# Last pooled queries as quarter products, diagonals by one GpSimd multiplication, and a new written-out order

## The chip, the cores and the metric

The kernel runs on one NeuronCore of a Trainium2 chip. The metric is the device time of one execution in microseconds; lower is better. The time of a kernel is the median of several executions. The engines are named as in the profile: PE is TensorE (PEld its loading of weights), DVE is VectorE, ACT is ScalarE, POOL is GpSimd, SP is SyncE, which here issues all DMAs.

## What is computed

Eight batches of eight heads, 576 positions, 64 elements per head. Each head goes through two attentions, whose sum is the input of a mixing layer:

```python
q_d = q.reshape(B, H, S // 4, 4, D).mean(axis=3)      # k_d, v_d likewise
out_up = np.repeat(sm_attn(q_d, k_d, v_d), 4, axis=2)  # attention among 144 pooled positions
mask = np.abs(pos[:, None] - pos[None, :]) < 4         # local attention, 7 keys per query
out_local = softmax(where(mask, q @ k.T / 8, -1e9)) @ v
x = (out_up + out_local) as (B, S, 512)
xk = mu_k * x + (1 - mu_k) * x_prev                    # xr likewise with mu_r
out = sigmoid(xr @ w_r) * (relu(xk @ w_k) ** 2 @ w_v)
```

All arrays are float32. The weights are 512x512 (`w_r`), 512x1024 (`w_k`) and 1024x512 (`w_v`).

## The kernel before, in words

Two heads make a pair; there are 32 pairs (n = 0 to 31), four to a batch. Positions of all batches are 4608 rows, cut into ten chunks of 512 or 256 rows (c = 0 to 9). A chunk needs the attention output of its rows, so pairs run ahead of chunks and both are interleaved on TensorE.

**A pair.** q and k are loaded (`load_raw`, L489) and turned; for pairs 0 to 4 TensorE turns them (`flip`, L537), later VectorE. GpSimd pools four neighbours of q into `qd` (`pool_q`, L589), of k into `kd` (`pool_k`, L604), and of v into `vd` (`pool_v`, L614). `score_pe` (L636) makes the local scores in many small matmuls: 96 passes for a pair below 8, 48 from pair 8 on. The pooled scores are 144 queries by 144 keys for each head e. Queries 0 to 127 come from `down_part_pe` (L711), four 64x64 products for the four quarters of the array (e is the quarter's rows, h its columns; "D" in the lists below). The last 16 queries come in one of two ways: for pairs 0 to 8 `last_q` (L597, ScalarE, two copies) puts them beside zeros in columns 144 to 271 of `qd`, and `down_last` (L706) makes one product with all 128 rows, two passes (line 709); for later pairs `down_part_pe` with h = 2 takes queries 80 to 143 of each head as two more quarter products ("L").

**Quarters.** `quarters(n, m, last)` (L822) makes four lists, one for each quarter of the array, with the value products of pair n (W: 48 columns, U and T: 144 columns) and the pooled scores of pair m (D, L). It issues them interleaved by planned time, so that the four quarters work side by side. With `last` true the L entries are left out. Softmax then goes over VectorE, ScalarE and GpSimd (`down_top`, `down_exp`, `down_sum`, `down_norm`, `score_top` to `spread`); `down_turn` (L754) turns the result back for pairs below 8. `av_out` (L887) writes the pair's part of x.

**Who calls them.** `score_both` (L852) for pairs 0 to 4 makes `down_last`, scores, four quarters; `down_alone` (L858) does so without scores for pair 8; `run_pe` (L863) makes a run of scores of pair n with values of pair n-1: for n = 5 to 7 in the order `down_last`, quarters, scores; from 8 on scores, quarters with L.

**A chunk.** `mix_prev` and `mix_part` form xk and xr, `mix_high` and `mix_low` split them into two parts for full accuracy; `k_pe` (L951), `v_pe` (L997) and `r_pe` (L983) are 12, 6 and 12 matmuls of up to 512 columns. The first chunk's xk is made on TensorE by `mix_pe` (L931) from eight diagonal matrices 128x128 that `diagonals` (L405) makes on ScalarE from the identity and `mus`; `mus` come from `load_mus`, `turn_mus` (TensorE) and `copy_mus` (ScalarE). The 20 weight parts (`fetch_weight`, 512 KB each) are split by `weight_scale` to `weight_low` (L447 to L481).

**Order.** Every step is added to a plan (`Plan.add`, L142) with its engine, an estimated time and a due time. `ORDER` (L47) is a written-out order of all 1995 steps: two characters for one step, its number in order of adding. `arrange` (L273) takes it, assigns PSUM banks, and computes planned times; each engine then issues its own steps in that order, five queues in all. `fill` (L333) puts throw-away matmuls (`keep_warm`, L471, line 475) where the plan has TensorE wait in the first 100 us. A queue never overtakes: a step that waits holds all behind it on its engine.

Of the kernel before, what the change touches and what calls it, by code (L numbers as in the profile page):

```python
# [17 lines left out]
P = 128  # L18
# [65 lines left out]
OtOuOvOwO)O*O-O4O3OxOyO,O+O/O.
# [9 lines left out]
class Plan:  # L94
# [18 lines left out]
    GROW = dict(DVE=1.03, ACT=1.02, POOL=1.05, SP=1.1)  # L113
# [244 lines left out]
def attention_moe(ctx: ExitStack, tc, q, k, v, mu_k, mu_r, w_k, w_v, w_r, band, ident, out):  # L358
# [14 lines left out]
    qds = [cp.tile([P, 272], F32, name=f"qd{i}") for i in range(2)]  # L373
# [332 lines left out]
    def down_last(n):  # L706

        d = st[n]
        nc.tensor.matmul(down_boards[n][:, D0 + DP:D0 + DP + 144], d["qd"][:, 144:272], d["kd"], start=True, stop=True)

# [7 lines left out]

    def down_pe(n):
        for e in range(2):  # L720
            for h in range(2):
                down_part_pe(n, e, h)
# [637 lines left out]
```

## Time and profile before

| | us |
|---|---|
| median of 3 runs | 652.75 |
| lowest and highest | 652.3, 652.94 |
| the profiled execution | 653.26 |
| its span, first to last instruction | 651.1 |

| engine | busy us of the span | share |
|---|---|---|
| PE | 631.3 | 97% |
| PEld | 519.5 | 80% |
| DVE | 443.7 | 68% |
| ACT | 421.3 | 65% |
| POOL | 315.4 | 48% |

Matmuls overlap in the array and their ends are modelled, so TensorE's busy time says when it stood still, not how well it was used. The profile gives for a stretch each engine's busy time, and TensorE's granted clock (1.00 is 2.4 GHz, 0.50 is 1.2 GHz). A wait is put down to what ended last before it; "issue" is a wait for which the profile shows no cause.

### The profile page before, as it was taken

To read this page: it belongs to the slowest core of one execution; us is meant where nothing else is said; L and a number is where in the kernel's file an instruction comes from. 1 tells how busy PE (TensorE), PEld (TensorE's weight loads), DVE (VectorE), ACT (ScalarE), POOL (GpSimd) and SP (SyncE) were. 2 spreads that over 40 slices of the span, in tenths; PEclk is the share of its full clock that TensorE was granted. 3 is DMA by queue.
4 is the path that set the end of the run, shared out by engine and by line. 5 is a ranking of instruction groups with operands and counts; after the bars stand their busy time and mean duration, and the time that the engine had idled before them with its cause. 6 is when DMAs were issued, how large, how long until landed. Compare 5 with 4: busy or idle time off the path is not lost.

```text
span 651.1 us, 18025 instructions
## 1 busy us (share of the span) xinstructions
PE 631.3 (97%) x6970; PEld 519.5 (80%) x6970; DVE 443.7 (68%) x892; ACT 421.3 (65%) x959; POOL 315.4 (48%) x462
## 2 busy tenths in 40 slices
PE   6989989999999999999999999999999999999997
PEld 5676777887887888788888888888887888888886
DVE  3978766699589887975477777798569754522313
ACT  4987855686669566755776775776576765752442
POOL 5477888856654636633435356457455541000000
PEclk9989989999999999999999999999999999999999
DMA  7898968355556544665226646646553530010001
GB/s 259 281 249 137 235 121 157 73 98 105 128 106 146 126 87 92 127 151 107 56 55 132 143 89 131 121 86 144 116 106 76 130 67 13 17 49 0 29 6 65
DMA packets 251575, 71.91 MB, mean 110 GB/s; under 512 B 224346, under 2 KB 243170, under 8 KB 251490
## 3 DMA queue, kind: packets, MB, share of 16 engines
q1 hardware_dynamic: 251490, 70.76, 48.5%
q8 instruction: 55, 0.90, 0.6%
q14 instruction: 30, 0.25, 0.1%
HBM read 56.85 MB, written 13.86 MB: 109 GB/s over the span
## 4 chain that ended last, share of the span: by engine, by line
PE 69%; DVE 11%; DMA 8%; SPq 4%; ACT 3%; issue 3%; POOL 2%; DVEq 0%; POOLq 0%; ACTq 0%
PE ps_g L957 26%; PE acc L1005 23%; PE ps_r L989 9%; PE ps_v L806 5%; DVE mix L927 4%; DMA wk<-in_moe_w_k_dram 3%; PE ps_a L646 2%; DMA v<-in_v_dram 2%; SPq L500 1%; DVE xks L949 1%; PE ps_a L715 1%; DMA keys<-blocks 1%; PE ps_f L545 1%; SPq L781 1%; DMA kraw<-in_k_dram 1%
## 5 line engine op out<-in xcount | busy, mean ns | idle before, releaser
L957 PE MATMUL ps_g<-xks,wk 128*128 128x512 f32 (+1 forms) x960 | 207.3, 370 | 2.3 <-DVE xks L949 1.4
L957 PEld LDWEIGHTS ps_g<-xks,wk 128*128 128x128 f32 x960 | 167.8, 188 | 35.1 <-DVE xks L949 2.3
L1005 PE MATMUL acc<-wv,kh 128*128 128x512 f32 x578 | 181.4, 395 | 0.0
L1005 PEld LDWEIGHTS acc<-wv,kh 128*128 128x128 f32 x578 | 106.9, 189 | 21.9
L1005 PE MATMUL acc<-wv,kl 128*128 128x512 f32 x289 | 113.0, 391 | 0.3 <-DVE kl L977 0.3
L989 PE MATMUL ps_r<-wr,xr 128*128 128x512 f32 x432 | 103.3, 390 | 0.0
L989 PEld LDWEIGHTS ps_r<-wr,xr 128*128 128x128 f32 x432 | 80.6, 188 | 17.4 <-DVE xr L949 0.4
L927 DVE SCALAR_TENSOR_TENSOR mix<-xt,mus,mix 128x256 f32<-128x256 f32 (+3 forms) x184 | 87.3, 516 | 9.4 <-ACT mix L922 9.1
L977 DVE TENSOR_TENSOR kl<-kk,kh 128x512 fp32r<-128x512 f32 (+1 forms) x63 | 43.3, 688 | 63.9 <-ACT kh L970 57.8
L752 POOL TENSOR_TENSOR an<-ad,sd 64x144 f32<-64x144 f32 (+2 forms) x128 | 70.6, 562 | 22.2 <-DVE sd L743 12.3
L922 ACT ACTIVATE mix<-xt,mus 128x256 f32<-128x256 f32 (+3 forms) x184 | 71.0, 443 | 7.2 <-DVE xr L949 3.4
L964 ACT ACTIVATE kk<-ps_g 128x512 f32<-128x512 f32 (+1 forms) x80 | 43.5, 547 | 47.3 <-PE ps_g L957 45.1
L977 POOL TENSOR_TENSOR kl<-kk,kh 128x512 fp32r<-128x512 f32 (+1 forms) x17 | 21.8, 1281 | 96.2 <-ACT kh L970 95.3
L1005 PEld LDWEIGHTS acc<-wv,kl 128*128 128x128 f32 x289 | 54.6, 189 | 12.4 <-DVE kl L977 0.7
L970 ACT ACTIVATE kh<-kk 128x512 fp32r<-128x512 f32 (+1 forms) x80 | 47.1, 589 | 24.7 <-PE acc L1005 22.7
L689 POOL TENSOR_TENSOR sm<-sm,ssum 128x384 f32<-128x384 f32 x32 | 28.9, 902 | 70.4 <-DVE ssum L685 58.3
L674 POOL TENSOR_TENSOR sm<-sm,mx 128x384 f32<-128x384 f32 x28 | 24.1, 861 | 69.9 <-DVE mx L669 69.8
L806 PE MATMUL ps_v<-bd,vw 64*64 64x48 f32 x1536 | 51.5, 217 | 0.0
L610 POOL TENSOR_TENSOR tk<-kz 64x288 f32<-64x288 f32 (+1 forms) x56 | 39.3, 701 | 18.0 <-DMA keys<-blocks 8.5
L806 PEld LDWEIGHTS ps_v<-bd,vw 64*64 64x64 f32 x1536 | 47.4, 134 | 0.0
L969 ACT ACTIVATE kk<-kk 128x512 f32<-128x512 f32 (+1 forms) x80 | 46.6, 583 | 1.0
L736 ACT ACTIVATE ad<-ps_a,mxd 128x144 f32<-128x144 f32 x96 | 35.1, 375 | 15.4 <-DVE mxd L728 9.7
(110 smaller groups left out, 982.2 us busy)
## 6 DMA issues: line engine op xcount, KB each, us to landing
vw<-in_v_dram SPq DMA_DIRECT2D x126, 96.0 KB, 2.8
out_dram<-sig SPq DMA_DIRECT2D x35, 256.0 KB, 2.5
v<-in_v_dram SPq DMA_DIRECT2D x32, 256.0 KB, 3.0
qraw<-in_q_dram SPq DMA_DIRECT2D x108, 72.0 KB, 2.7
kraw<-in_k_dram SPq DMA_DIRECT2D x108, 72.0 KB, 2.6
wk<-in_moe_w_k_dram SPq DMA_DIRECT2D x8, 512.0 KB, 5.9
wv<-in_moe_w_v_dram SPq DMA_DIRECT2D x8, 512.0 KB, 5.7
keys<-blocks SPq DMA_DIRECT2D x96, 40.0 KB, 1.8
```

Of the source, the lines that this page charges most:

```text
L610: nc.gpsimd.tensor_tensor(out=tk[h], in0=k4[:, :, 0:2], in1=k4[:, :, 2:4], op=ALU.add)
L752: nc.gpsimd.tensor_tensor(out=x, in0=y, in1=z, op=ALU.mult)
L806: nc.tensor.matmul(pv[r][64 * e:64 * e + 64, cols], lhs, rhs, start=(i == 1), stop=(i == NG + 1 + (r != e)))
L922: nc.scalar.activation(mixes[c, h, nm][:, p, o:o + L], xts[b][:, p, s:s + L], AF.Copy, scale=rest)
L927: nc.vector.scalar_tensor_tensor(out=to[:, p, o:o + L], in0=xts[b][:, p, s + 1:s + 1 + L], scalar=mu[:, p:p + 1], in1=to[:, p, o:o + L], o ...
L957: nc.tensor.matmul(ps, w_k_part(p, f, w), x[:, :, y, p, :], start=(m == 0), stop=(m == len(mm) - 1))
L964: nc.scalar.activation(kk, kq[c, f].rearrange("p h t -> p (h t)"), AF.Relu)
L969: nc.scalar.activation(kk, kk, AF.Square)
L970: nc.scalar.activation(kh, kk, AF.Copy)
L977: eng.tensor_tensor(out=kl, in0=kk, in1=kh.bitcast(F32), op=ALU.subtract)
L989: nc.tensor.matmul(ps, x[:, y, p, o:o + P], ws[f"r{p}"][:, w, :], start=(m == 0), stop=(m == len(mm) - 1))
L1005: nc.tensor.matmul(accs[c, t][:, j], x[:, o:o + P], ws[f"v{f}"][:, w, j], start=(f == 0 and m == 0), stop=(f == NF - 1 and m == 2), skip_g ...
```

## The change

The last queries of pairs 0 to 8 go the same way as those of later pairs: `last_q`, `down_last` and `down_pe` are gone, `qd` has 144 columns instead of 272, and `score_both`, `down_alone` and `run_pe` call `quarters` with `last` false. In runs 5 to 7 the scores now come ahead of the quarters. The eight diagonals are one GpSimd multiplication of the identity with `mus`, both broadcast. `ORDER` is another list, of 1986 steps (nine `last_q` fewer; `diagonals` on GpSimd). Some planned times differ, which acts on the issued program only through the places of the throw-away matmuls, the PSUM banks and a few waits of SyncE's queue for earlier transfers: 1.2 instead of 1.1 as SyncE's factor, q and k from pair 5 on 2.1 instead of 2.0 us of DMA, `load_v4` 1.9 instead of 1.7.

```diff
-    qds = [cp.tile([P, 272], F32, name=f"qd{i}") for i in range(2)]
+    qds = [cp.tile([P, 144], F32, name=f"qd{i}") for i in range(2)]
...
     def diagonals(nm):
         diags[nm] = wp.tile([P, NP, 2, P], F32, tag="f32tmp", name="diag", bufs=2)
         a = 0 if nm == "xk" else 1
-        for p in range(NP):
-            for j in range(2):
-                nc.scalar.activation(diags[nm][:, p, j, :], idn, AF.Copy, scale=mus[:, a + 2 * j, p:p + 1])
+        by = mus.rearrange("p a n -> p n a")[:, :, a::2]
+        nc.gpsimd.tensor_tensor(out=diags[nm], in0=idn[:, None, None, :].broadcast_to([P, NP, 2, P]),
+                                in1=by[:, :, :, None].broadcast_to([P, NP, 2, P]), op=ALU.mult)
...
-    def last_q(n):
-
-        qd = qds[n % 2]
-        for e in range(2):
-            h = slice(64 * e, 64 * e + 64)
-            nc.scalar.activation(qd[h, 192 + 64 * e:208 + 64 * e], qd[h, 128:144], AF.Copy)
...
     def score_both(n):
         score_tile(n, n)
-        down_last(n)
         score_pe(n)
-        down_pe(n)
+        quarters(None, n, False)
 
     def down_alone(n):
         score_tile(None, n)
-        down_last(n)
-        down_pe(n)
+        quarters(None, n, False)
 
     def run_pe(n):
         m = n + 1 if n >= EARLY else n
         score_tile(n, m)
-        if n < SPLIT:
-            down_last(m)
-            quarters(n - 1, m, True)
-            score_pe(n)
-        else:
-            score_pe(n)
-            quarters(n - 1, m if m < n1 else None, False)
+        score_pe(n)
+        quarters(n - 1, m if m < n1 else None, False)
...
-        if n <= EARLY:
-            add("ACT", 0.43, R - 6, last_q, n, w=[f"qd.{i}"])
...
-        add("ACT", 2.44, MU + 20, diagonals, "xk", r=["mu", "idn"], new=[("diagxk", "f32tmp")])
+        add("POOL", 2.2, MU + 20, diagonals, "xk", r=["mu", "idn"], new=[("diagxk", "f32tmp")])
```

The start of the two orders, decoded for two queues (k, q: `load_raw`; w: `fetch_weight`; v: `load_v4`; win: `load_windows`):

```
TensorE before: flip 0q 0k 1q 1k, score_both 0, weight_diff 0 4 2 1, flip 2q, weight_diff 3, turn_mus, score_both 1, flip 2k
TensorE after:  flip 0q 0k 1q, score_both 0, flip 1k 2q, weight_diff 3, score_both 1, turn_mus, flip 2k, weight_diff 1 4
both, later:    down_turn 3, mix_pe 1, av_pe 3, mix_pe 2 3, down_turn 4, k_pe(0,0), run 5
SyncE before: consts q0 k0 w0 q1 w2 k1 w4 w1 w3 q2 w10 w13 mus w7 w5 k2 q3 v0 k3 w19 v1 q4 win0 w8 w11 k4 w6 v2 win1 w16 w17 win2 v3 win3
SyncE after:  consts q0 k0 w4 q1 w3 w1 k1 q2 w0 w2 w10 mus k2 w5 v0 q3 w8 w13 k3 q4 w7 v1 w19 k4 win0 w6 w16 v2 win1 w11 win2 v3 win3
```

## Rows read from the trace of the kernel before

**Rows 1.** The page, part 1: busy us, share of the span, instructions of each engine.

```profile
PE 631.3 (97%) x6970; PEld 519.5 (80%) x6970; DVE 443.7 (68%) x892; ACT 421.3 (65%) x959; POOL 315.4 (48%) x462
```

**Rows 2.** Windows: stretch, its length, engines' busy us, granted clock, DMA share, GB/s.

```profile
core 0: us, PE busy (x) PEld busy (x) DVE busy (x) ACT busy (x) POOL busy (x), PEclk, DMA share, GB/s
20.00:30.00 10.00, 9.61 (x196) 6.40 (x194) 9.14 (x20) 9.92 (x27) 6.42 (x12) 1.00 0.90 282
30.00:40.00 10.00, 8.15 (x270) 7.33 (x269) 9.74 (x22) 9.82 (x29) 8.53 (x14) 1.00 0.93 270
31.00:42.20 11.20, 9.11 (x291) 8.32 (x291) 10.06 (x23) 9.61 (x29) 10.55 (x16) 1.00 0.90 267
45.70:68.00 22.30, 21.73 (x456) 15.02 (x455) 20.20 (x49) 17.86 (x51) 17.41 (x28) 1.00 0.86 169
93.44:96.85 3.41, 3.41 (x20) 2.70 (x9) 3.16 (x8) 0.52 (x1) 2.04 (x3) 0.50 0.52 83
205.00:600.00 395.00, 393.35 (x3877) 325.60 (x3876) 275.54 (x554) 258.55 (x560) 171.11 (x247) 1.00 0.44 94
```

**Rows 3.** Timeline of TensorE, run 6: start us, us, engine, line, tiles, count.

```profile
88.58 0.41 PE L709 MATMUL ps_a<-kd,qd 128*128 128x144 f32 x2
88.92 0.33 PE L806 MATMUL ps_v<-adT,vd 64*64 64x144 f32 x1
...
90.50 0.61 PE L651 MATMUL ps_a<-kz,qT 64*32 64x32 f32 x47
```

**Rows 4.** The chain of waits in order of time: start us, us, what.

```profile
38.92 1.75 issue
...
91.11 1.81 issue
...
93.54 4.51 PE acc L1005 x12
...
109.95 1.14 issue
...
125.44 0.62 PE ps_v L806 x16
...
127.01 2.97 PE acc L1005 x12
```

**Rows 5.** Timeline of TensorE, score_both of pair 4 and the next work.

```profile
54.36 0.49 PE L709 MATMUL ps_a<-kd,qd 128*128 128x144 f32 x2
54.79 1.02 PE L651 MATMUL ps_a<-kz,qT 64*32 64x32 f32 x96
55.74 0.48 PE L715 MATMUL ps_a<-kd,qd 64*64 64x144 f32 x8
56.19 0.30 PE L806 MATMUL ps_v<-adT,vd 64*64 64x144 f32 x1
```

**Rows 6.** Groups by line, ScalarE's steps that leave: busy us, mean ns, idle before.

```profile
L602 ACT ACTIVATE qd<-qd 64x16 f32<-64x16 f32 x18 | 3.8, 210 | 0.1
...
L410 ACT ACTIVATE diag<-idn,mus 128x128 f32<-128x128 f32 x8 | 2.4, 386 | 0.0
```

**Rows 7.** Waits of TensorE's weight loads, 5 to 68 us: total us, times, longest.

```profile
PEld ps_w L469 <- ACT wk L462: 1.0, 3, 0.4
...
PEld ps_f L545 <- ACT wk L479: 0.8, 1, 0.8
```

**Rows 8.** View of one line, L728 and L484: duration ns min/median/max.

```profile
L728 DVE TENSOR_SCALAR mxd<-mxd x32: 168/172/954, 20.5 to 521.2; 128x3 f32<-128x3 f32 x32
...
L484 POOL TENSOR_TENSOR wv<-w,wv x8: 1265/1284/1304, 32.3 to 102.7; 128x512 fp32r<-128x512 f32 x8
```

**Rows 9.** Timelines of GpSimd and VectorE from 28.4 to 29.5 us.

```profile
28.43 1.00 POOL L619 TENSOR_TENSOR v<-v 128x384 f32<-128x384 f32 x1 [0.97 <-DMA v<-in_v_dram]
...
28.67 0.78 DVE L728 TENSOR_SCALAR mxd<-mxd 128x3 f32<-128x3 f32 x1
```

**Rows 10.** The page, part 3: instruction queue: packets, MB, share of 16 engines.

```profile
q8 instruction: 55, 0.90, 0.6%
```

More of the change, by code (lines that the diff above doesn't have):

```diff
@@ new lines @@
+4z1c3K0+2>0)2$3C363V2%3b0*3c3W1a152&3l3D3o3E3X3F3G3r3m3d3e3u3n4$3Y3Z3p3q3w3y163s3&3a3t3;3T3f4&4%3z3g4(1b1d3!3h
+1e1f1g3<3#3v3(0,3=0-4*571K1Q4/4+4:4058181i4!4#0.5B4;4,501h4-173>4.444<4=480/1L411R1S1M421T5152531N5C5D434>1U3+
+4549191j0:543,1A551k565E4)4b4a4d4c3x1B1l5G464A1V475X595Y4B5b5K5H5d5F5!5I5J5L1O1P4f4e4C5Q5M5c5R3-1m1C5S4D3)4E5T
+5N5U4G4H4h5e1D5x5A5V5z5$4F5y5a5;5Z5#3.3*5W5O5P4g5g3$4I5h5k5l5i5j4i4j4K5<5q5=7m5.7n5%4J5f5>5m605r5s5t4L5n5u7;7j
+4M4O5&4P62615:4N1n5o4l4k5v5w5(5p5)5*3%634Q646E656F5+667p687r4R6L6G6P6N694m4n4S4U6R4T3/6H6Q5,6A6O6M6S3:4p4o6I4V
@@ new lines @@
+6T6V6U6Z6f6J7o6l6j4Y6K6h4Z6g4r6m6k6i4W7.5/7k7/5-677<6B7q7s6W6C6b6n6o4X6z7t6!6X6a4t6c4q7&7l7:7(6%6<6.7)7>7=7y7*
+6D8N7x8O8L8l4v807+6Y6#6&7z7,7u7!7v7w6d7-81824s6$6e7#836p84857$6*6(6+6)8D8E6/8F6t6r7L7M7D7N7O7%4u8Q876,6v888P8G
+8R8H6-896w8I7E8J6=8S8A7P7Q6:8K868T6>8U6;8B8o8p8CAL8e8V8W8r8q8Y8M8f8n8g8t7S7R708h71757T7U8Z728s8i6s8j768k738a8b
+6u6q748c8X8u8v778(8)8*AMAIAk8dAK8m4w4x8yAn8w8x8/AO8z8+8=787W7V7F798;906x8!8>8:8<917A6y8#AJ927B7CAQ8,8-93ANAoA.
+7G947Y7X7J7Z7H9A9E9G9K9I9B8.9F967c7b959H9J9L978$AP9M7IAR7a8%9NAS7K98AT7e99Ad9CAq9D9Y9Z9a9bAXAeAUAfAg9c9k9&9d9O
@@ new lines @@
+AYApAZA;8&AWAsAhArAiAl7f7gA<AjAV7dAt9)Aa9eAu9(9U9*Ab9fAvA&A(AmAwA=9VAy9/9:9gAcAxA)9SA*A+B09QAz9hA>A,9<9;9lA-9i
+B1B2A!A#9jB39m9RA$B4B59P9TBNBOA/7hA%9>9=BPBD9nBEA:B7BQ9oBFBG9W9pB89qBRBHBI9rB9BSBA7iB6BKD!D#BMA0A19sA2A39tBJ9u
+9X9vBBBTBUBVBWBlD%BeBrBpBYBfBCEADxBLDyBXBvBnBxD$BwA5A49w9!Bg9xBmBsBqBo9yBZ9zBh9#BtBu9-A7A69$9%9+A8A9D(D&BiB(B.
+B*B,B#B)ByB+B$B/9.BzB-BjBk9,B:B;D)D*ADB!C7C8C9B%DzD,ABD+AACBCCCDBaE0D/E1B&D-B<C1C3C,B=CAECB>E2ACC0EBEbE7AFBbE3
+BcBdCJCFClCmCGCECNCnCoE4E9C.D:CKCHEDE5E6D;D.EYCICRCqCpCOC<CLEFD<CMEECSCPD=E8D>AEEcEZC/C=EGEHEICsCrEJC-CQCTCfCg
@@ new lines @@
+ELERESC:ETCdCVCWCuCtCZCUCvCwEeEdC4C2EaEUEfEgEVC5CeEMC6EWENC;D1EXCaCXCbEOCYEPEKE$EzE!E%GZAGEhEiCcEsEjEkE&EQAHEl
+EtEuEvEmEwD2ExE(C>EnD5D3D7EyCyCxCjCzC!ChE)CkCiE*E#D4C$D6D8D0EoC%E+E,E-E.D9F8DADFDBDNGaGWC)GyF1EpF2GYFIE:GbGdFJ
+G#GXDCFAFODDFEE;C#F9DEFBDGH7C*C(EqFPE<DHFCDIFDC&FFErE/E=DhDJDjDKFMF3FKDkGcFLFGFHDlDRDmDdDLDiFSFYFWDMF4DOFUF5DP
+DQDSDnDZDVGeGiDoDTFTF6FVF7DWFZDUFNFXDaFaFbFQE>GfDpGrG%FmG!GsGgDXDYDbDqDeFRFcFdGhGlDcGtGmG$HAC+G&FnDfFqDrG0F0HB
+GzGkH8G)GnGuGvDgG(GwGjGoDsGxFrFoG*FsDtDuGpFpFtH0FgG1GqG.HYDvHbHZG2G3H1HDG/H2G+G:FuFyFvFiFzHFG8G9G,H3G-HCHcH4G;
@@ L85 @@
+NUNXNVN=O0O2O1NYNZNzNaNyNbNcNeN#NdO3N!N%N4NfN>O4O5NgNhOGN$OHN6LsLvLuLtNlNiN7N8N9N5NANjOKOLOIOJN(N&N*N)OqOOOMON
+OaOrNBO6OPOQOROSOTOUOCOVOsO8OWOXOYOtOAObOcOZO9O7ODOBOdNmOuNoNnNpOEOeOfOgOvOiOFOhN,OwOmOjOkOlOxOoN.N-OnOpOyN+N/
+O#N:OzO!O$O%
 """
@@ L112 @@
     ISSUE, LAND = 0.6, 2.2
[L113 removed]
+    GROW = dict(DVE=1.03, ACT=1.02, POOL=1.05, SP=1.2)
     QUEUE = 5.2
@@ L704, in score_tile @@
         down_boards[m] = boards[n]
-    def down_last(n):
-        d = st[n]
-        nc.tensor.matmul(down_boards[n][:, D0 + DP:D0 + DP + 144], d["qd"][:, 144:272], d["kd"], start=True, stop=True)
     def down_part_pe(n, e, h):
@@ L717, in down_part_pe @@
                          start=True, stop=True)
[L719 to L722, printed above, removed]
     def down_top(n):
@@ L1079, in down_steps @@
         R1 = at_run[n] if n >= EARLY else after(n)
-        add("DVE", 0.8, R1 - 14, down_top, n, r=[ps], w=[f"mxd{n}"], lock=ps)
+        add("DVE", 0.9, R1 - 14, down_top, n, r=[ps], w=[f"mxd{n}"], lock=ps)
         add("ACT", 1.2, R1 - 13, down_exp, n, r=[ps, f"mxd{n}"], w=["ad"], lock=ps)
@@ L1179, in places @@
             W = where[f"k{f}"]
-            add("PE", 1.62 if n == 1 else 2.9, W, k_pe, c, f,
+            add("PE", 1.59 if n == 1 else 2.88, W, k_pe, c, f,
                 r=[x for h in range(n) for x in parts_of("xk", c, h)] + both(f"k{4 * (f // 4) + p}" for p in range(NP)),
@@ L1190, in r_part @@
                 h = t // 2
-                add("PE", 2.89, where[f"r{t}"], r_pe, c, t,
+                add("PE", 2.88, where[f"r{t}"], r_pe, c, t,
                     r=parts_of("xr", c, h) + both(f"r{p}" for p in range(NP)), new=[(f"r{c}.{t}", "bank")])
@@ L1198, in v_part @@
                     ts = (2 * h, 2 * h + 1)
-                    add("PE", 1.55, where[f"{'vw'[h]}{f}"], v_pe, c, h, f, r=[f"kh{c}.{f}", f"kl{c}.{f}"] + both([f"v{f}"]),
+                    add("PE", 1.52, where[f"{'vw'[h]}{f}"], v_pe, c, h, f, r=[f"kh{c}.{f}", f"kl{c}.{f}"] + both([f"v{f}"]),
                         new=[(f"acc{c}.{t}", "bank") for t in ts] if f == 0 else [],
```

55 lines of the change are left out of this document (16 added, 39 removed).

## The prediction

> **What bounds the kernel now.** I read the page first, then ten-microsecond windows, then the waits, the chain and the timelines of the places that the diff touches. The page shows TensorE busy for 97% of the span, the other engines for 48 to 68% [rows 1]. The windows show where the missing 3% lies: from 205 to 600 us TensorE stands idle for 1.65 us of 395, from 45.7 to 68 us for 0.57 of 22.3, from 31 to 42.2 us for 2.09 of 11.2 [rows 2]. So nearly everywhere the end is set by TensorE's own work, and an edit pays in one of three ways: it takes work off TensorE, it ends one of the few idle stretches, or it spares TensorE a stretch at the lower clock. Only in the first 40 us are others as full: ScalarE is busy 9.92 and 9.82 of 10 us there [rows 2].
>
> The profiled execution took 653.26 us (span 651.1 and 2.2 around it), 0.5 above the median of 652.75; I subtract from the median.
>
> **Term 1, the full-width product leaves runs 5 to 7.** `down_last` is one product with all 128 rows, two passes. In run 6 it begins at 88.58 and the next work at 88.92: 0.34 us on the bounding engine [rows 3]. The same 16 queries now go to the quarter lists as two 64x64 products ("L"). There they cost nothing: lists (0,0) and (1,1) have one long product fewer than (0,1) and (1,0), so L fills a hole. Rows agree: run 6 without L takes 1.58 us for its quarters (88.92 to 90.50) [rows 3], run 8 with L 1.57 (125.44 to 127.01) [rows 4]. Three runs give -1.0 us. That scores now come ahead of the quarters adds nothing: no wait of TensorE for the quarters' inputs shows in the chain there, and they get about 1 us more of time.
>
> **Term 2, six calls without values.** In `score_both` (pairs 0 to 4) and `down_alone` the lists hold no values, so L cannot hide. Before, in pair 4: 0.43 us for `down_last` with the start of the scores behind it (54.36 to 54.79), of which I count the 0.34 of run 6, and 0.45 for the four quarters (55.74 to 56.19) [rows 3, 5]. After: the four quarters and a second round. A round is two passes like `down_last`'s own, so it costs at least nothing (both fit the drain of the first) and at most another 0.45. I take 0.24, the planner's value for a long product, which lies between. Saved: 0.34 - 0.24 = 0.1 each, -0.6 in six; ends -2.0 and +0.7.
>
> **Term 3, ScalarE's relief in the head.** Eight diagonal products of 386 ns and 18 copies of 210 ns leave ScalarE [rows 6], five pairs' copies and all diagonals from the first 60 us: some 4.5 us. It can pay only where TensorE waits for ScalarE; from 5 to 68 us the two largest such waits are 1.0 and 0.8 us [rows 7]. So the term lies between 0 and -1.8; VectorE is as full (9.74 of 10 [rows 2]) and takes over part of it, so I take the middle, -0.9. The halved clearing of `qd` runs before the first input lands and is worth nothing; without that cover it would be a gain, too small to count.
>
> **Term 4, the diagonals on GpSimd.** One multiplication over 128x1024 elements. GpSimd takes 1284 ns for 128x512 and 1.00 us for 128x384 [rows 8, 9]: 2.57 to 2.67 us, about the 2.4 of ScalarE [rows 6], on an engine that has 1.5 us in 10 free where ScalarE has 0.2 [rows 2]. Decoded, the new list puts it 8th on GpSimd, ahead of `pool_k(2)`, `pool_v(0)`, `pool_q(2)` and `score_norm(0)`; they wait if `copy_mus` is late. That step has moved from ScalarE's place 33 to 18, so I expect it in time. Cost 0; if the cover fails, up to 2.6.
>
> **Term 5, the new order.** Decoded list against list, TensorE's first 37 steps are the same set, with 14 weights instead of 15 fetched ahead of `load_windows(3)` on SyncE's queue (weight 17 now follows). A weight is 512 KB, at 267 GB/s [rows 2] 2.0 us earlier for pairs 3 and 4. TensorE hides that: it is idle for only 0.57 us there [rows 2]. Against it, pair 1's k now stands behind one weight more, 2.0 us; `score_both(0)` has been put ahead of its flip to cover it. After 205 us the order can win at most 1.65 us and can lose any amount; I take 0, ends -1.5 and +1.3.
>
> Sum: -1.0 - 0.6 - 0.9 + 0 + 0 = -2.5, 650.2 us.
>
> **What the sum leaves open: TensorE's instruction supply.** The chain has three idle pieces put down to "issue" that are long: 1.75, 1.81 and 1.14 us, all within dense runs of small matmuls, two of them in runs 6 and 7 [rows 4]. The page's instruction queue moved 55 packets for 13,940 matmuls and weight loads [rows 1, 10], one per 253. A run of 5 to 7 issues 332 (336 after) in about 3 us, more than one packet, so I read these as waits for the next packet. After the one at 91.11 the granted clock is 0.50, the lower of its levels, from 93.44 to 96.85 [rows 2], where twelve value products took 4.51 us instead of 2.97 [rows 4]: 1.81 + 1.54 = 3.35 us for one wait with its clock. The edits move every packet boundary by some matmuls, so such a wait may vanish or appear; I put 0 in the sum and 3.35 on both sides.
>
> The Trainium skill ("Runtime: NRT & Kernel Launch", Instruction fetch mechanics) says that instructions come in 16 KiB blocks of 256 and that crossing a block is mostly hidden. By that page nothing could come or go here, and the sum would stand without this bound; the trace's 1.81 us speaks against it.
>
> **The rivals.**
> *A. The multiplication holds VectorE.* A 3-element VectorE step began at 28.67, inside a GpSimd product that ran from 28.43 to 29.43, and took 0.78 us, to 29.45, instead of its median 172 ns [rows 8, 9]. So the small VectorE steps of softmax can be held until a GpSimd operation ends, now one of 2.6 us. Price: 2.5 us if VectorE's queue is what TensorE waits for just then: 652.7, no change. Against it: the step must fall into the first part of the multiplication, and GpSimd's other steps held it before as well.
> The Trainium skill ("SBUF — State Buffer", SBUF: two separate sides) has this as a lock on a shared pair of ports for the whole instruction; the trace agrees with 0.78 against 0.17 us.
> *B. A supply wait goes.* The one at 91.11 does not recur, nor its clock: 650.2 - 3.35 = 646.8. For it: in the list the packet boundary in run 6 shifts only slightly, but arrival times shift by more.
> *C. Slower: one supply wait more.* Run 5, 6 or 7, or the head's `av_pe` calls, cross a boundary before the packet is there; it decides once the packet takes longer than 253 instructions last, some 3 us. With terms 1 and 2 only, the head's gain lost: 652.75 - 1.6 + 3.35 = 654.5.
> *D. Nothing gained.* The head's relief is eaten by VectorE and new bubbles take the 1.6: 652.8. For it: 395 us that are already solid can only get worse.
>
> **How the numbers follow.** A measurement of this kernel tells about 0.2% from no change: 651.4 to 654.1. Forecast (648.6 to 651.4) 0.45; A 0.08; B 0.17; C 0.16; D 0.14. Faster: 0.43 of the forecast and B make 0.60. Same: A, D 0.22. Slower: C and a rest, 0.18. Time 650.2. The range takes in B (and 0.8 below, for term 2's better end) and C: 646.0 to 654.8; beyond it lie about 2 in 10, two waits gone or two more.
>
> **What would show it.** No line 709, 384 quarter passes where there were 348, quarters in runs 5 to 7 at 1.58 us with no step ahead of them: term 1. ScalarE's waits on TensorE's side below 1 us by 68 us, and the first `k_pe` no later than 68.0: term 3. One GpSimd multiplication near 2.6 us, with no VectorE step stretched beside it: term 4 right, A wrong. "Issue" pieces near 1.1 and 1.8 us and one half-clock stretch after 68 us: the supply as before; none is B, two half-clock stretches are C. I am wrong if the first `k_pe` moves by over 2 us, or idle time between 122 and 600 us changes by over 1.5.

## The result, and the profile after

The changed kernel takes 645.55 us (median of 20 executions) against 652.67 for the kernel before, measured beside it: the ratio is 0.990, 95% interval 0.988 to 0.992, so 5 to 8 us less. The ratio on record is estimated from the fast runs alone and is not the quotient of the two medians, which is 0.989. I forecast 650.2 in 646.0 to 654.8. The direction was right and the gain about two and a half times the forecast one: the ratio on the 652.75 that the forecast started from is 646.4, just inside the range, and the median itself just below it.

The profiled execution took 645.42 us, its span 643.6 (before 653.26 and 651.1). First the page, part 1:

```profile
span 643.6 us, 18025 instructions
...
PE 626.3 (97%) x6984; PEld 514.5 (80%) x6984; DVE 449.0 (70%) x892; ACT 415.1 (65%) x933; POOL 311.5 (48%) x463
```

TensorE is busy 5.0 us less and stands idle 2.5 us less than before [rows 1], with 14 matmuls more. The windows of the changed kernel say where:

```profile
20.00:30.00 10.00, 9.56 (x151) 6.34 (x151) 9.03 (x20) 7.43 (x21) 7.83 (x12) 1.00 0.93 315
...
31.00:42.20 11.20, 10.47 (x290) 7.75 (x288) 10.70 (x20) 10.08 (x25) 8.94 (x15) 1.00 0.92 233
45.70:68.00 22.30, 21.73 (x405) 14.61 (x407) 20.96 (x46) 17.72 (x50) 17.96 (x27) 1.00 0.90 182
66.00:122.00 56.00, 55.05 (x839) 44.97 (x839) 40.96 (x80) 36.00 (x89) 49.72 (x66) 1.00 0.76 160
122.00:205.00 83.00, 81.40 (x900) 66.65 (x899) 71.64 (x143) 57.27 (x132) 48.10 (x71) 1.00 0.59 119
205.00:600.00 395.00, 393.93 (x3777) 326.67 (x3776) 272.21 (x542) 256.75 (x554) 165.45 (x243) 1.00 0.43 91
```

and for the two stretches that [rows 2] does not have, the windows of the kernel before:

```profile
66.00:122.00 56.00, 52.80 (x709) 43.99 (x708) 38.64 (x75) 37.10 (x93) 47.01 (x62) 0.97 0.72 158
122.00:205.00 83.00, 81.86 (x902) 67.14 (x901) 66.49 (x136) 56.21 (x136) 52.81 (x74) 1.00 0.52 107
```

The first number behind the length is TensorE's busy time. From 66 to 122 us its idle time falls from 3.20 to 0.95 us and the granted clock rises from 0.97 to 1.00; after 122 us idle time is 1.60 + 1.07 us where it was 1.14 + 1.65, no difference.

Two instructions serve as milestones: the first product of `k_pe` and the first of `r_pe`, in the views of one line (count, duration ns min/median/max, first and last start). Before:

```profile
L957 PE MATMUL ps_g<-xks,wk x960: 277/389/501, 68.0 to 638.4; 128*128 128x512 f32 x154, 128*128 128x256 f32 x38
...
L989 PE MATMUL ps_r<-wr,xr x432: 387/389/501, 129.8 to 646.5; 128*128 128x512 f32 x144
```

After:

```profile
L933 PE MATMUL ps_g<-xks,wk x960: 274/389/506, 64.6 to 630.9; 128*128 128x512 f32 x154, 128*128 128x256 f32 x38
...
L965 PE MATMUL ps_r<-wr,xr x432: 387/389/504, 122.6 to 639.0; 128*128 128x512 f32 x144
```

The head (up to the first `k_pe`) is 3.4 us shorter, the middle, with runs 5 to 7 in it, 58.0 us instead of 61.8, and from there to the last product of `r_pe` it is 516.4 us instead of 516.7. So 7.2 of the 7.5 us are won before 123 us, about half in the head and half in the middle, as far as this one pair of executions goes.

The middle is where the supply waits stood. Run 6 on TensorE after the change (start us, us, count; scores L644, quarters L789 and L703, then the chunk's products L981):

```profile
86.48 1.02 PE L644 MATMUL ps_a<-kz,qT 64*32 64x32 f32 x96
87.43 0.33 PE L789 MATMUL ps_v<-adT,vd 64*64 64x144 f32 x1
...
89.15 0.73 PE L981 MATMUL acc<-wv,kh 128*128 128x512 f32 x2
```

The 96 score passes go through in one piece; before, 1.81 us of "issue" stood between pass 47 and the rest [rows 3, 4]. The waits of TensorE from 66 to 122 us (us in total, times, longest) sum it up. Before:

```profile
PE ps_a L651 <- issue: 3.0, 2, 1.8
```

After:

```profile
PE acc L981 <- DVE w L457: 0.8, 1, 0.8
```

Both supply waits of the middle are gone, and with them the stretch at the lower clock from 93.44 to 96.85 [rows 2]: 3.0 us of waits and half of the stretch's 3.41 make 4.7 us. A new wait gives back 0.8: a weight part. The chain of waits shows it behind two transfers of `wv`, which the new order fetches later:

```profile
62.76 7.22 DMA wv<-in_moe_w_v_dram
69.99 6.61 DMA wv<-in_moe_w_v_dram
...
80.13 0.64 DVE w L457
...
80.81 5.74 PE acc L981 x24
```

The net of 3.9 is the middle's 3.8 us, within what these rows resolve. The head of the changed kernel is not free of such waits; it has two (timeline of TensorE):

```profile
14.55 1.20 PE L545 MATMUL ps_f<-idn,kraw 64*64 64x64 f32 x33 [1.20 <-issue]
...
20.44 0.61 PE L644 MATMUL ps_a<-kz,qT 64*32 64x32 f32 x46 [1.07 <-issue]
```

### The profile page after: what moved, and what is told of

It is laid out like the page before. It is cut to its first block, busy times and chain, and to the rows that moved or that the text cites. A ratio compares the mean times of both kernels' runs of the same rounds, so it can differ in the third digit from the quotient of the medians.

```text
span 643.6 us, 18025 instructions
## 1 busy us (share of the span) xinstructions
PE 626.3 (97%) x6984; PEld 514.5 (80%) x6984; DVE 449.0 (70%) x892; ACT 415.1 (65%) x933; POOL 311.5 (48%) x463
## 4 chain that ended last, share of the span: by engine, by line
PE 84%; DVE 5%; DMA 2%; ACT 1%; SPq 1%; issue 1%; DVEq 0%; ACTq 0%
PE acc L981 30%; PE ps_g L933 29%; PE ps_r L965 13%; PE ps_v L789 6%; PE ps_a L639 3%; DMA wv<-in_moe_w_v_dram 2%; PE ps_a L703 1%; DVE mix L903 1%; PE ps_m L911 1%; DVE w L457 0%; DVE xks L925 0%; DMA vw<-in_v_dram 0%; DVE ps_w L453 0%; PE ps_a L644 0%; SPq L511 0%
## 5 line engine op out<-in xcount | busy, mean ns | idle before, releaser
L981 PE MATMUL acc<-wv,kh 128*128 128x512 f32 x578 | 180.3, 393 | 0.8 <-DVE w L457 0.8
L981 PEld LDWEIGHTS acc<-wv,kh 128*128 128x128 f32 x578 | 106.2, 188 | 23.3 <-DVE w L457 1.3
L981 PE MATMUL acc<-wv,kl 128*128 128x512 f32 x289 | 112.5, 389 | 0.0
L953 DVE TENSOR_TENSOR kl<-kk,kh 128x512 fp32r<-128x512 f32 (+1 forms) x63 | 44.6, 709 | 63.1 <-ACT kh L946 63.0
L735 POOL TENSOR_TENSOR an<-ad,sd 64x144 f32<-64x144 f32 (+2 forms) x128 | 66.0, 525 | 31.7 <-DVE sd L726 21.8
L981 PEld LDWEIGHTS acc<-wv,kl 128*128 128x128 f32 x289 | 54.2, 188 | 11.9 <-DVE kl L953 0.4
L789 PE MATMUL ps_v<-bd,vw 64*64 64x48 f32 x1536 | 51.5, 217 | 0.0
L789 PEld LDWEIGHTS ps_v<-bd,vw 64*64 64x64 f32 x1536 | 47.4, 134 | 0.0
L682 POOL TENSOR_TENSOR sm<-sm,ssum 128x384 f32<-128x384 f32 x32 | 30.2, 945 | 30.2 <-DVE ssum L678 21.9
```

The lines of the kernel that those rows point to most:

```text
L735: nc.gpsimd.tensor_tensor(out=x, in0=y, in1=z, op=ALU.mult)
L789: nc.tensor.matmul(pv[r][64 * e:64 * e + 64, cols], lhs, rhs, start=(i == 1), stop=(i == NG + 1 + (r != e)))
L953: eng.tensor_tensor(out=kl, in0=kk, in1=kh.bitcast(F32), op=ALU.subtract)
L981: nc.tensor.matmul(accs[c, t][:, j], x[:, o:o + P], ws[f"v{f}"][:, w, j], start=(f == 0 and m == 0), stop=(f == NF - 1 and m == 2), skip_g ...
```

## The experiments

Theory S says that the supply waits hang on where dense work stands in the program, counted in instructions. Against it stood that the new order, or the new sequence within a run, removed them. For the head the question was whether the new code or the new order shortened it. In all kernels with "lead" throw-away products stand ahead of the work, so that every later TensorE instruction stands further in the program by the number in the name: a product is two instructions, a weight load and a matmul. Ratios are to the kernel before, measured beside each on the same chip, with 95% intervals; the experiments ran on three chips, so medians of different rows compare less well than ratios. lead10 has only 6 executions, and its medians alone give 0.991 (647.27 to 653.13). The last two columns are those of one profiled execution: k_pe is the first `k_pe` in it, "runs 5 to 7" the "issue" waits there.

| kernel | median us | ratio | k_pe | runs 5 to 7 |
|---|---|---|---|---|
| changed | 645.55 | 0.990 [0.988, 0.992] | 64.6 | none |
| lead10 | 647.27 | 0.988 [0.985, 0.992] | 64.8 | none |
| lead150 | 654.11 | 1.001 [0.998, 1.003] | 66.8 | 3.20, 0.85 |
| diag_act | 647.12 | 0.992 [0.990, 0.995] | 70.0 | none |
| quarters_first | 648.44 | 0.992 [0.989, 0.995] | 64.2 | 2.02 |
| first_lead64 | 648.28 | 0.994 [0.991, 0.996] | 66.8 | none |
| parts_only | 650.62 | 0.996 [0.993, 0.998] | 70.6 | none |
| parts_lead10 | 650.38 | 0.996 [0.994, 0.999] | 70.9 | none |
| parts_lead100 | 650.10 | 0.996 [0.993, 0.999] | 67.1 | none |
| order_only | 651.42 | 0.997 [0.995, 0.999] | 67.9 | 1.44 |
| order_lead10 | 651.77 | 0.999 [0.996, 1.002] | 66.4 | 1.33 |
| order_lead100 | 651.82 | 0.999 [0.996, 1.001] | 68.0 | none |
| before_lead28 | 651.24 | 0.997 [0.995, 0.999] | 65.9 | 1.16 |

One execution is not the kernel: before_lead28's profile (648.26 us) is of the fastest of its 12 executions, diag_act's (650.45) of the slowest of its 11. What the record has of every execution is the mean granted clock. In the profiled ones it is 0.997 or less where the trace has a stretch at the lower level ahead of the last microseconds, and 0.999 or more where it has none; 0.998 is counted as none here. By this mark a stretch is in 57 of 96 executions of the kernel before (those beside the experiments), in 6 of 20 of the changed kernel, in none of lead10's 6 and in all 12 of lead150. Without one, the medians are 651.7 us before (39 executions) and 645.4 for the changed kernel (14): 6.3 of the 7.1 us remain, so the lower clock is the smaller part of the gain. The groups were made after the fact, and no other execution's waits are on record.

**lead10 and lead150: the changed kernel, moved within its program.**

```diff
+    def lead(count, cols):
+        z = cp.tile([P, 512], mybir.dt.bfloat16, name="z")
+        nc.vector.memset(z, 0.0)
+        ps = pp.tile([P, 512], F32, tag="b5", name="ps_x", bufs=1)
+        for _ in range(count):
+            nc.tensor.matmul(ps[:, 0:cols], z[:, 0:128], z[:, 0:cols], start=True, stop=True)
+
+    in_order(lead, 5, 480)
```

(lead150: 75 products of 32 columns.)

> The changed kernel with 5 throw-away products of 480 columns ahead of TensorE's first work (10 instructions, 2400 columns), in time where TensorE waits for data anyway. It is the control of lead150, which streams as many columns. Theory S: as the changed kernel or up to 2 us faster, if the clock rises earlier; no wait for instructions longer than 0.5 us in runs 5 to 7. Rival (the long issue pieces have nothing to do with where the packet boundaries lie): the same.

> The changed kernel with 75 throw-away products of 32 columns ahead of the first work (150 instructions, 2400 columns). It moves every packet boundary 140 instructions against lead10: in runs 5 and 6 then two boundaries lie within one run (44th and 300th, 73rd and 329th instruction). Theory S: a wait of 1 us or more put down to issue in both runs, near their ends, and often a half-clock stretch after them: 2 to 7 us slower than lead10. Rival (position has nothing to do with it): within 1 us of lead10.

Neither the work nor its order differs between the two, only the place in the program, and the gain is there in one and gone in the other. lead150's timeline of TensorE in runs 5 and 6 (idle time before an instruction in brackets):

```profile
71.78 0.45 PE L703 MATMUL ps_a<-kd,qd 64*64 64x144 f32 x5
75.43 0.42 PE L789 MATMUL ps_v<-bd,vw 64*64 64x48 f32 x9 [3.20 <-issue]
...
94.91 0.42 PE L703 MATMUL ps_a<-kd,qd 64*64 64x144 f32 x3
96.17 0.37 PE L789 MATMUL ps_v<-bd,vw 64*64 64x48 f32 x5 [0.85 <-issue]
```

Both stand near the ends of their runs, as expected, the second a little shorter than the 1 us that I asked for. The window behind the first shows the lower level again:

```profile
76.70:80.11 3.41, 3.41 (x10) 2.64 (x9) 3.26 (x10) 2.25 (x8) 1.19 (x3) 0.50 0.95 339
```

That is rival C on the chip: 3.20 + 0.85 + 1.7 = 5.8 us in the middle. lead150 took 6.8 us more than lead10, in the expected 2 to 7. Here theory S holds: the new order and sequence alone do not keep the waits away. In lead10 no "issue" wait of over 0.2 us is left in the head, where the changed kernel has 1.20 and 1.07 at 14.6 and 20.4 us; its first `k_pe` is no earlier. These two early waits cost nothing that shows in this pair of profiles.

**before_lead28: the kernel before, moved by 14 products.** Its `z` is the cleared `kz` here (171 columns).

> The kernel before, untouched but for 14 throw-away products of 171 columns ahead of TensorE's first work: 28 instructions more, so every packet boundary lies 28 instructions earlier in the work. In run 7 it moves from the 41st to the 13th instruction, in run 6 from the 239th to the 211th, with 28 slow instructions more between the asking for a packet and its use. Theory S: no issue piece over 0.5 us in runs 5 to 7 and no half clock after 68 us; from the first k_pe to the first r_pe 57.5 to 59 us where before took 61.8; the whole 2 to 5 us faster than before, by added work alone. Rival (only what the change edits counts): within 1 us of before.

Of the two supply waits in the middle one is left, in run 7. Before, run 7:

```profile
109.09 0.86 PE L651 MATMUL ps_a<-kz,qT 64*32 64x32 f32 x76
111.09 0.32 PE L651 MATMUL ps_a<-kz,qT 64*32 64x32 f32 x20 [1.14 <-issue]
```

and before_lead28, run 7:

```profile
103.94 0.74 PE L651 MATMUL ps_a<-kz,qT 64*32 64x32 f32 x62
105.84 0.43 PE L651 MATMUL ps_a<-kz,qT 64*32 64x32 f32 x34 [1.16 <-issue]
```

Fourteen products ahead, and the wait comes after 62 score passes instead of 76: exactly 14 earlier. It stands at a fixed instruction of the program, whatever work is there. Run 6's wait did not come at all in this execution, so the place says where a wait can be, and not whether it comes. I had expected none in run 7 either, since its boundary moved to the 13th instruction; I had overlooked that a run of 332 instructions has a second boundary 256 further on, and there the wait came.

The traces say more. I count TensorE's instructions from the start of the program: matmuls, weight loads and its few semaphore instructions, throw-away products included. Then every one of the 38 "issue" waits of over 0.3 us in the 14 kernels stands behind 449 instructions and a whole multiple of 256 more, whatever the code and the order. Behind 3777 (449 + 13 x 256) the kernel before, before_lead28, order_only, order_lead10 and quarters_first wait in run 7. Of the waits put down to another instruction or a load only one, in diag_act, stands at such a place. The transfers of the instruction queue are on record one by one too: each of the 38 waits ended 1.0 to 1.8 us after one had landed. In run 6 before, the transfer lasted from 90.58 to 91.54, and work went on at 92.92. So these are waits for packets of 256 instructions, as the prediction read them.

The kernel as a whole gained 0.1 to 0.6%, where I had expected 2 to 5 us (0.3 to 0.8%) and the rival less than 1: the time does not tell them apart. From the first `k_pe` to the first `r_pe` the profiled execution took 58.8 us, within the expected 57.5 to 59. Its head gained too, without any edit and at the full clock up to there, 2.1 of the 3.4 us that the change won there:

```profile
L957 PE MATMUL ps_g<-xks,wk x960: 274/389/504, 65.9 to 633.3; 128*128 128x512 f32 x154, 128*128 128x256 f32 x38
```

**quarters_first and first_lead64: does the sequence within a run matter?** Runs 5 to 7 of the changed kernel with the quarters ahead of the scores, and the same moved by 32 products of 75 columns.

```diff
-        score_pe(n)
-        quarters(n - 1, m if m < n1 else None, False)
+        if n < SPLIT:
+            quarters(n - 1, m, False)
+            score_pe(n)
+        else:
+            score_pe(n)
+            quarters(n - 1, m if m < n1 else None, False)
```

> The changed kernel with quarters ahead of the scores again in runs 5 to 7, L products kept. Theory: quarters issued behind the 64-row scores start out of step and lose 0.15 to 0.3 us of what the missing down_last gives; put first, runs 5 to 7 take 2.53 us each instead of 2.76 to 2.91, 0.7 us in all, too little to be told in the time. Rival (the L products cost what down_last did): the runs stay at 2.76 or more.

> The changed kernel with quarters first in runs 5 to 7 and 32 throw-away products of 75 columns at the start (64 instructions), which puts the boundaries of runs 5, 6 and 7 near the middle of the run or outside it. Theory S: no issue piece over 0.5 us in runs 5 to 7; 643 to 646.5 us, 0 to 2 us below the changed kernel, with a smaller spread between executions. Rival: as the changed kernel.

quarters_first has a wait again in run 7, with the lower clock from 106.18 on:

```profile
102.02 0.76 PE L644 MATMUL ps_a<-kz,qT 64*32 64x32 f32 x65
104.79 0.36 PE L644 MATMUL ps_a<-kz,qT 64*32 64x32 f32 x31 [2.02 <-issue]
```

first_lead64 has none there, but took 648.28 us where I expected 643 to 646.5: in its head stands a wait of 2.59 us at 24.17 us, with a stretch at the lower clock behind it, and by its granted clock every one of its 12 executions has such a stretch. The wait had moved, and not gone. In the table, with the quarters ahead (quarters_first, first_lead64, order_only and its two, before, before_lead28) five of seven builds wait in runs 5 to 7; with the scores ahead (all others) one of seven does. Whether the sequence itself makes waits rarer, or seven places fell well, is open. The ratios of both kernels overlap with the changed one's: no version here has beaten it.

**diag_act: the changed kernel with the eight diagonals on ScalarE again,** at the same place in the list.

```diff
-        by = mus.rearrange("p a n -> p n a")[:, :, a::2]
-        nc.gpsimd.tensor_tensor(out=diags[nm], in0=idn[:, None, None, :].broadcast_to([P, NP, 2, P]),
-                                in1=by[:, :, :, None].broadcast_to([P, NP, 2, P]), op=ALU.mult)
+        for p in range(NP):
+            for j in range(2):
+                nc.scalar.activation(diags[nm][:, p, j, :], idn, AF.Copy, scale=mus[:, a + 2 * j, p:p + 1])
```

> The changed kernel with the eight diagonals back on ScalarE, at the same place of the list. TensorE's instructions and packet boundaries are unchanged, so this is the diagonals' part alone. Theory S: ScalarE has room (7.43 us of 10 from 20 to 30 us), so 0 to 1 us slower, first k_pe at 64.5 to 65.5 us. Rival R (ScalarE's relief shortens the head): 2 us or more slower, first k_pe after 66.5 us.

The ratio's interval overlaps with the changed kernel's, so what the multiplication is worth by itself is not told apart from nothing. The first `k_pe` at 70.0 us is what rival R asked for, but in this execution, the slowest of the kernel, a wait of 1.84 us ends at 55.85 us, with 6.83 us at the lower clock behind it. The profile puts it down to a value load, but it stands behind 2241 instructions (449 + 7 x 256), where six other kernels wait for supply, so it is probably one of these waits. This `k_pe` does not tell what the diagonals are worth.

**parts_only, and order_only.** The first is the new code with the old order (its nine `last_q` taken out); the second the new order with the old code, each `last_q` put right behind its `pool_q`.

parts_only against the changed kernel is the old list with the old planned times, seven lines of them (SyncE's factor and the times of q, k, v, `down_top`, `k_pe`, `r_pe` and `v_pe`), of which the section on the change names the first three; order_only against the changed kernel:

```diff
...
         score_tile(n, n)
+        down_last(n)
         score_pe(n)
-        quarters(None, n, False)
+        down_pe(n)
...
-        score_pe(n)
-        quarters(n - 1, m if m < n1 else None, False)
+        if n < SPLIT:
+            down_last(m)
+            quarters(n - 1, m, True)
+            score_pe(n)
+        else:
+            score_pe(n)
+            quarters(n - 1, m if m < n1 else None, False)
...
+        if n <= EARLY:
+            add("ACT", 0.43, R - 6, last_q, n, w=[f"qd.{i}"])
...
-        add("POOL", 2.2, MU + 20, diagonals, "xk", r=["mu", "idn"], new=[("diagxk", "f32tmp")])
+        add("ACT", 2.44, MU + 20, diagonals, "xk", r=["mu", "idn"], new=[("diagxk", "f32tmp")])
```

The four others have the throw-away products of their names ahead (10: five products, 100: fifty).

> The old order with the new code: last queries as quarter products, diagonals by one GpSimd multiplication, nothing moved. Theory S (the gain is the new order, mostly through TensorE's waits for instructions and its clock; the code parts themselves are worth about 1 us): 649.5 to 652, that is 1 to 3 us below before. Counting matmuls and weight loads, the packet boundary in run 7 moves from its 41st to its 13th instruction, so the wait of 1.14 us in run 7 should be gone; the one in run 6 may stay. Rival R (ScalarE's relief and the free L products are what shortened the first 65 us): 4 us or more below before, first k_pe before 65.5 us.

> The new order with the old code: down_last, last_q (put right behind pool_q on the list) and the diagonals on ScalarE, at the places where the new list has them. Theory S: 3 to 6 us below before, 646.5 to 649.5, first k_pe at 65 to 66.5 us. Rival R: within 2 us of before.

> The old order with the new code (last queries as quarter products, diagonals by GpSimd), with five throw-away products of 480 columns ahead of everything: all later TensorE instructions stand 10 further in the program. Theory P (the new code itself shortens the first 70 us by 1 to 1.5 us, and what parts_only lost there, its issue waits of 1.21, 1.19 and 1.86 us and its 6.83 us at the lower clock, hangs on places in the program): the issue waits change place or size, and the first k_pe less the issue waits before it and less half of the time at the lower clock before it comes to 62.5 us, plus or minus 0.7 (parts_only 62.5 by the same working, before 63.8). Theory O (only the new order shortens the first 70 us): it comes to 63.8 or more. From the first k_pe to the end 578 to 579 us in both, unless runs 5 to 7 wait for supply.

> As parts_lead10 with fifty throw-away products of 48 columns: all later instructions stand 100 further. A second place for the same question. Theory P: the corrected first k_pe (less issue waits and half of the time at the lower clock) again at 62.5 plus or minus 0.7, with other waits than in parts_only. Theory O: 63.8 or more.

> The new order with the old code, and five throw-away products of 240 columns ahead of the first load's work: later instructions stand 10 further. Theory P: the first k_pe less issue waits and half of the time at the lower clock stays near 66 us (order_only 66.3), since down_last, put where the new order puts score_both, waits for kd (1.76 us at 12.4 us in order_only). Theory O: it comes near 62.5. Whether run 7 again waits for supply (1.44 us and 3.41 us at the lower clock in order_only) is open; without it the time should be about 648.3.

> As order_lead10 with fifty products of 48 columns: later instructions stand 100 further. Theory P: corrected first k_pe near 66 us; theory O: near 62.5. The supply waits move again.

*The new code alone* gives 0.4% at all three places: 2.4 to 2.9 us, what I forecast for the whole change. It has no supply wait in runs 5 to 7, but pays in the head, each time: "issue" waits of 4.7, 4.6 and 3.5 us in all, and in parts_only and parts_lead10 6.8 us at the lower clock from about 45 us on (parts_lead10 has 3.4 us of it earlier as well). By the granted clock 11 of 12 and 10 of 12 executions of these two have a stretch, 6 of 12 of parts_lead100. The window of that stretch in parts_only (granted clock behind the five engines), and then the timeline of TensorE in parts_lead100:

```profile
44.69:51.52 6.83, 6.83 (x141) 5.83 (x138) 3.80 (x11) 5.02 (x12) 5.70 (x12) 0.50 0.95 216
```

```profile
41.08 0.51 PE L545 MATMUL ps_f<-idn,qraw 64*64 64x64 f32 x10 [3.52 <-issue]
...
44.21 1.26 PE L545 MATMUL ps_f<-idn,kraw 64*64 64x64 f32 x36 [1.36 <-ACT qT L552]
```

The wait for ScalarE's copy of qT (1.33 to 1.36 us near 44 us) is in all three; the changed kernel does not have it.

*The new order alone* gives 0.1 to 0.3%, at two of three places not told from nothing. I had expected 3 to 6 us of it, first `k_pe` at 65 to 66.5; order_only took 651.42 us, within 2 us of before, with `k_pe` at 67.9. So the half of theory S that gave the gain to the order is not borne out. It moves the waits with the program, as before_lead28 did. In order_only run 7 waits after 71 score passes, in order_lead10, five products on, after 66; in order_lead100 no run from 5 to 7 waits (timelines of TensorE, first order_only, then order_lead10).

```profile
107.75 0.81 PE L651 MATMUL ps_a<-kz,qT 64*32 64x32 f32 x71
109.99 0.33 PE L651 MATMUL ps_a<-kz,qT 64*32 64x32 f32 x25 [1.44 <-issue]
```

```profile
106.21 0.77 PE L651 MATMUL ps_a<-kz,qT 64*32 64x32 f32 x66
108.32 0.35 PE L651 MATMUL ps_a<-kz,qT 64*32 64x32 f32 x30 [1.33 <-issue]
```

Beside that it has waits of the old code that no shift removes. `down_last`, ahead of the scores, needs `kd` at once, 1.76, 2.23 and 1.45 us near 12.4 us; and run 7 waits 1.56 to 1.58 us for adT. The timelines of order_only, first TensorE, then ScalarE in run 7:

```profile
12.38 0.51 PE L709 MATMUL ps_a<-kd,qd 128*128 128x144 f32 x2 [1.76 <-POOL kd L611]
...
106.05 0.33 PE L806 MATMUL ps_v<-adT,vd 64*64 64x144 f32 x1 [1.58 <-ACT adT L796]
```

```profile
103.70 0.44 ACT L602 ACTIVATE qd<-qd 64x16 f32<-64x16 f32 x2 [2.64 <-POOL qd L595]
104.15 0.96 ACT L700 ACTIVATE bd<-at,side 128x288 f32<-128x288 f32 x2
105.02 0.98 ACT L796 ACTIVATE adT<-ps_t 128x288 f32<-128x288 f32 x3
```

ScalarE stands at `last_q` for GpSimd's `qd`, and adT, which TensorE needs, is queued behind. That place for `last_q` was mine; an order that was searched for the old code would put it elsewhere. So the two parts do not add up, 0.4 + 0.2 against 1.0%. That the order is one for this code may be a reason, but it is not shown; the lower clock is another. Executions without a stretch at it have medians of 646.5, 648.1 and 648.2 us with the new code alone (1, 2 and 6 executions) and 651.1, 650.0 and 650.6 with the new order alone (6, 7 and 6), that is 3.5 to 5.2 and 0.6 to 1.7 us below the 651.7 of before, against 6.3 for both together. Among these few executions the parts come near to adding up, and the new code is the larger one.

*Theories P and O for the head.* The first `k_pe` less "issue" waits and less half of the time at the lower clock came to 61.2 and 63.6 us in the two parts kernels, 66.4 and 64.9 in the two order kernels. O fails in all four; P is nearer, but three of the four lie outside what it allowed. The working was at fault: lead10 shows that a wait early in the head can vanish without the head becoming shorter, so they can't just be subtracted. What the rows do show is that neither part alone, in six builds, has its first `k_pe` before 66.4, and that both together have it at 64.2 to 64.8 in the three builds that keep the full clock up to there. Even that is of single executions, and it says little for the two parts: before_lead28, with neither of them, has 65.9.

## Why the prediction was right in its direction and short in its size

**The step that failed is the one that left the supply at 0.** I had its mechanism, its places and its price of 3.35 us per wait with its clock. But I called the forecast case without it the likeliest (0.45), and gave rival B only 0.17, conceding that "the packet boundary in run 6 shifts only slightly". The runs show that a slight shift is all it takes: 10, 28, 64, 100 or 150 instructions moved, removed or brought back waits in the shifted kernels above. That the supply would stay as it was should have been the less likely case, and the sum should have been given for none, one and two waits. B's 646.8 is for one wait gone; in the profiled execution both went, 4.7 us, and 0.8 came back as a wait for `wv`. How often they go in other executions is not on record.

So the size was in part luck of the place. The changed kernel at three places (changed, lead10, lead150) has a mean ratio of 0.993, the kernel before at two (itself and before_lead28) of 0.9985: by these five, an estimate, the change is worth about 3.5 us wherever it stands, nearer the forecast 2.5 than the 7.1 measured.

By the signs that I had set, what came is rival B, with no long "issue" piece behind 68 us. One sign of being wrong came too: the first `k_pe` moved by 3.4 us, and I had allowed 2. So the head is not explained by the sum either.

**Term 1 was mis-sized.** I took -0.34 for each of runs 5 to 7 since the quarters' 1.58 us would stay. Run 6 after: quarters 87.43 to 89.15, 1.72 us, 0.14 more; the 64-row scores begin 0.32 us behind the chunk's last product (101.15 to 101.47 in run 7), where `down_last` began 0.23 behind. Left is 0.34 - 0.14 - 0.09 = 0.11 each, -0.3 in all. "That scores now come ahead of the quarters adds nothing" was the wrong sentence: behind the 64-row scores the lists took longer, I take it because they start out of step. With the quarters ahead, run 7 of first_lead64 takes 2.87 us from the start of the chunk's last product before it to the first behind it (102.93 to 105.80), against 2.99 in the changed kernel (101.15 to 104.14), 0.12 us and a little less than the 0.15 to 0.3 that I expected of quarters_first.

**Term 2 was right.** The second round of quarters costs little: line L703's 12 passes of one pair run from 32.37 to the next work at 33.02, 0.65 us, against 0.34 + 0.45 before [rows 3, 5]: -0.14 each, -0.1 forecast. The passes are 384, as forecast.

**Terms 3 and 5 are not told apart.** ScalarE's relief is there: 7.43 us from 20 to 30 where it had 9.92 [rows 2]. TensorE's wait from 31 to 42.2 us fell from 2.09 to 0.73, but 1.75 of the 2.09 was the supply wait at 38.92 [rows 4]. The bound of 1.8 us was read off the wrong engine row: it is idle time of the weight loads [rows 7], which overlap the matmuls, and the matmuls themselves waited for ScalarE only 0.43 + 0.34 us up to 68 us. The head gained 3.4 us where terms 2 and 3 gave 1.4 of it; supply waits and clock in the head fell from 2.6 + 1.7 us before to 2.3 after, which would be the rest, but the experiments do not show that such waits count in full. Past 122 us the order changed idle time by 0.1 us, within the 1.5 I allowed.

**Term 4 and rival A.** The multiplication was expected at 2.57 to 2.67 us and took 1.91. `copy_mus` was not quite in time: GpSimd stood still for 0.78 us before it. A's mechanism is there, in the timelines of GpSimd and VectorE:

```profile
22.37 1.91 POOL L409 TENSOR_TENSOR diag<-idn,mus 128x1024 f32<-128x1024 f32 x1 [0.78 <-ACT mus L403]
```

```profile
23.44 0.87 DVE L711 TENSOR_SCALAR mxd<-mxd 128x3 f32<-128x3 f32 x1
24.23 0.60 DVE L554 COPY kz<-ps_f 128x256 f32<-128x256 f32 x1
```

The three-element step began inside the multiplication and ended at 24.31, with the multiplication's end at 24.28: 0.87 us instead of about 0.17 [rows 8]. TensorE's waits up to 68 us have none for the steps behind it, so the cost of 0 stands. The Trainium skill's rule ("SBUF — State Buffer", SBUF: two separate sides) of a shared port pair held for a whole instruction agrees with these 0.87 us. Its other rule that I weighed ("Runtime: NRT & Kernel Launch", Instruction fetch mechanics), that crossing a block of instructions is mostly hidden, agrees with most of the 55 packets of the kernel before [rows 10], where five places show a wait of over 0.3 us, but not with those in dense runs: 3.20 us in lead150 were not hidden, and with the 0.85 and the lower clock they make most of its loss.

**Rivals C and D.** C did not come with the change but in lead150: one wait of 3.20 us with 1.7 of clock, 4.9 where 3.35 was worked out, and a second of 0.85. D fell: the stretch that was solid already lost nothing.

## What to carry to other kernels

Where small matmuls run densely for longer than one instruction packet lasts, look for idle pieces put down to "issue", and treat them as belonging to a place in the program: moving the work by a few throw-away instructions helps to tell whether a gain or a loss is the edit's or the place's. Time an edit at two or three such places before its worth is believed, and look at the granted clock of all executions before one profile is taken for the kernel. And a change of code and order may not split into its halves: here neither half alone gave more than 0.45%, both together 1%.

## What was not expected of the hardware

A supply wait moved by exactly as many passes as stood ahead of it (76 to 62 for 14, 71 to 66 for 5), and all 38 such waits stand whole multiples of 256 instructions apart in kernels of different code and order, while their length went from 0 to 3.5 us. The lower clock followed some of them and not others: 1.81 us in run 6 before, 1.44 in order_only and 3.20 in lead150 had it behind them, 1.33 in order_lead10 and 3.52 in parts_lead100 did not. And one GpSimd multiplication over 128x1024 with both inputs broadcast took 1.91 us, where two of the 128x512 steps that the estimate was made from would be 2.57 [rows 8].
